# A planner's books for VectorE and GpSimd: one port booked for both, and GpSimd's measured durations

## The chip, the core and the metric

The kernel runs on one core of a Trainium2 chip. The metric is the device time of one execution in microseconds (us); the profile adds the span, which is the time from the first to the last instruction of the program. The engines are TensorE (PE in the profile, PEld for its weight loads), VectorE (DVE), ScalarE (ACT), GpSimd (POOL) and SyncE (SP), whose queue issues most DMAs.

## What is computed

The reference is a dynamic convolution followed by a mixture of experts with one expert for each token. There are 8 sequences of 3584 tokens with 192 values each, which makes 28,672 tokens. Cut to what matters:

```python
w = softmax(weight_gen)                         # [B, S, 8 heads, 7 taps]
out[b,s,h,:] = sum_k w[b,s,h,k] * x_pad[b, s+k, h,:]   # causal, 24 values per head
x = out.reshape(28672, 192)
e = argmax(x @ w_gate)                          # one of 8 experts
gate = softmax(x @ w_gate)[e]
eom = sigmoid(x @ w_output_gate)
out[token] = gate * eom[e] * (relu(x[token] @ w1[e]) @ w2[e])   # 192 -> 1024 -> 192
```

## The kernel before

**The work.** The convolution and the routing are done in 32 units of 896 tokens (128 partitions with 7 tokens each), here called units 0 to 31. For each unit the kernel normalizes the 7 tap weights, forms 7 products of shifted tokens and weights ("taps", 128x1344 elements each), adds them up, splits the sum into a high and a low float16 part in a buffer `rt`, computes the logits of both gates on TensorE, ranks the tokens by expert, and scatters the rows to the DRAM table `srtd`, which is sorted by expert. The scatter is seven GpSimd indirect DMAs for a unit ("sends", `srtd<-rt,posi`).

The experts run on "tiles" of 512, 384, 256 or 128 sorted rows, 81 in all. For a tile SyncE loads the row data (`meta` and the transposed `xT`) and the expert's weights (`wa`, 1024 KB, and `wb`, 768.5 KB, whatever the size of the tile). TensorE runs the first product into PSUM in 2, 4 or 8 pieces. Of each piece ScalarE makes `hh` (relu, float16) and VectorE makes `hl`, the rest that `hh` lost ("evacuation"). TensorE then runs the second product, ScalarE scales it to `ys`, and GpSimd writes the rows to their tokens with an indirect DMA (`out_dram<-ys,meta`).

**Who does the taps.** For units 0 to 6 GpSimd makes four taps (`gap`) and VectorE three (`vap`), and TensorE adds them in PSUM. From unit 7 on GpSimd makes five, VectorE makes two whose weights lie in PSUM, and VectorE adds all seven in PSUM. In the first part VectorE also splits the eight experts' weights into halves (`wpa`, `wpb`), which go back to DRAM as `wd` before any tile can load them.

**What sets the order.** Nothing of the order is written by hand. Each strand of the work is a Python generator ("chain"). `Order.step` picks the chain that can go on earliest by the planner's own books, and of equals the one with the lower rank: evacuations first, then outputs, placing, rounds, the units, and the expert products last. Each engine is wrapped by a `Paced` object, which keeps a booked time `t` for it and adds an estimated duration to it for every recorded instruction (`vector_cost`, `gpsimd_cost` and so on). So the estimates set in which order each engine gets its instructions, and SyncE its DMAs. On the chip each engine then executes that fixed list in order and waits where data are missing. The estimate has no other effect: the number of taps, tiles and evacuations is the same whatever it says.

After unit 31 the tiles that are left are put in an order that spreads the sizes (`mixed`). At that point a further pool of buffers for weights is opened, and the last table asks for eight writes of padding rows to `srtd` by SyncE (`srtd<-pad`). Two of VectorE's small instructions in each unit read two operands in SBUF: `ps<-base,done` and `ps<-zt`.

Of the kernel before, what the change touches and what calls it, by code (L numbers as in the profile page):

```python
# [14 lines left out]
ALU = mybir.AluOpType  # L15
# [52 lines left out]
class Chain:  # L68


    def __init__(self, gen, rank, t, engine):
        self.gen, self.rank, self.t, self.engine, self.gate = gen, rank, t, engine, None
        self.slack = EAGER[1] if len(rank) > 1 and rank[0] in EAGER[2] and rank[1] < EAGER[0] else SLACK


class Order:


    def __init__(self):
        self.now, self.chains = 0.0, []  # L80
        self.cur = Chain(None, (), 0.0, None)

    def add(self, gen, rank, engine, t=None):
# [23 lines left out]
class Queue:  # L107
# [12 lines left out]
    def __getattr__(self, name):  # L120
        f = getattr(self.engine, name)

        def call(*args, **kwargs):
            c, own, issue = self.order.cur, self.cost(name, args, kwargs), self.issue(name, args, kwargs)
            r = f(*args, **kwargs)  # L125
            if self.host is not None:
                self.issued = max(self.host.t, c.t)
                self.host.t = self.issued + issue
            self.issued = max(self.issued, self.order.now) + issue
            if own is not None:  # L130
                self.moved = max(self.moved, self.issued + 0.65) + own
                c.t = max(c.t, self.moved + 1.0)
            return r

        return call


class Paced:


    def __init__(self, order, engine, cost, before=0.0, after=None, lead=0.0, follows=True):
        self.order, self.engine, self.cost, self.t = order, engine, cost, 0.0
        self.before, self.after = before, LAT if after is None else after
        self.lead, self.follows = lead, follows

    def __getattr__(self, name):
        f = getattr(self.engine, name)

        def call(*args, **kwargs):
            c, own = self.order.cur, self.cost(name, args, kwargs)  # L150
            r = f(*args, **kwargs)  # L151
            if own is not None:
                self.t = max(self.t, (c.t if self.follows else self.order.now) + self.before) + own
                c.t = max(c.t, self.t + self.after)
            return r

        return call


def largest(args, kwargs):  # L160

    best = 1
    for o in (*args, *kwargs.values()):
        n = 1
        for v in getattr(o, "shape", ())[1:]:
            n *= v
        best = max(best, n)
    return best
# [10 lines left out]

def gpsimd_cost(name, args, kwargs):  # L180
    if name == "indirect_dma_start":
        return 1.04
    if name == "memset":
        return 1.0
    return 0.06 + largest(args, kwargs) * (0.0022 if kwargs.get("op") == ALU.add else 0.00174)


def tensor_cost(name, args, kwargs):
# [22 lines left out]
def kernel(ctx: ExitStack, tc: tile.TileContext, x, wg, wgate, wogate, w1, w2, cst, out):  # L211
    nc = tc.nc
    od = Order()
    V = Paced(od, nc.vector, vector_cost)
    S = Paced(od, nc.scalar, scalar_cost, after=LAT_S)
    G = Paced(od, nc.gpsimd, gpsimd_cost)
    T_ = Paced(od, nc.tensor, tensor_cost, after=0.0)
    SP = Queue(od, nc.sync, sync_cost, sync_issue, LEAD)
    TQ = SP if TURN_SP else Queue(od, nc.scalar, sync_cost, sync_issue, LEAD, S)
# [64 lines left out]
    def has(u, *what):  # L284
        return lambda: all(k in U[u] for k in what)
# [73 lines left out]
    def scattered(ins):  # L359

        tc.declare_no_dep(ins.ins, group="srt", reason="rows of its own")
        tc.add_to_no_dep_group("srt", ins.ins)
        state["writers"].append(ins.ins.name)
# [11 lines left out]
    def scales(ssq, sc, inv, name, free=None):  # L375

        n = ssq.shape[1]
        ex = sp.tile([P, n], I32, tag=f"ex{n}", name=f"ex_{name}")
        V.tensor_scalar(ex, ssq.bitcast(I32), 1, MASK, op0=ALU.arith_shift_right, op1=ALU.bitwise_and)
        if free is not None:  # L380
            free.append(od.cur.t)
        yield V
        V.tensor_scalar(sc.bitcast(I32), ex, -1.0, float(197 << 23), op0=ALU.mult, op1=ALU.add)
        V.tensor_scalar(inv.bitcast(I32), ex, float(57 << 23), None, op0=ALU.add)

# [3 lines left out]
    def gate_steps():  # L389
# [12 lines left out]
        T_.matmul(pg[:, 0:1], lhsT=ones32, rhs=gss, start=True, stop=True)  # L402
        yield V
        sg = cp.tile([P, 1], F32, name="sg")
# [6 lines left out]
        S.activation(gm[:, :, 0:16], g2, AF.Copy, scale=sg)  # L411
        yield V
        V.scalar_tensor_tensor(out=gm[:, :, 16:32], in0=g2, scalar=sg, in1=gm[:, :, 0:16], op0=ALU.mult, op1=ALU.subtract)
# [387 lines left out]
    def place_steps(u):  # L801
# [29 lines left out]
        d["placed"] = True  # L831
        yield G, has(u, "weighed")
        od.cur.t = max(od.cur.t, d["weighed_t"])
        for j in range(JS):
            yield G
            scattered(G.indirect_dma_start(
                out=srtd[:, :], out_offset=bass.IndirectOffsetOnAxis(ap=posi[:, j : j + 1], axis=0),
# [98 lines left out]
    def tile_load(t, T, ti, i, writers, ka, kb):  # L936
# [36 lines left out]
    def gemm2_group(d, g, at):  # L973
# [6 lines left out]
        for f in range(8):  # L980
# [215 lines left out]
```

## Time and profile before

| what | value |
|---|---|
| median of 3 runs | 1299.13 us |
| the three runs | 1295.3, 1299.13, 1304.6 us |
| the profiled execution's own time | 1304.16 us |
| its span | 1302.4 us |
| granted TensorE clock, mean | 0.968 |

The profiled execution is thus 5.0 us (0.4%) above the median of the runs. The profile's page gives busy times of each engine, a row of 40 slices of the span for each, the costliest groups of instructions, and the chain of work that ended last. Almost all instructions have line 151 of the kernel, which is the wrapper that records them; groups are told apart by the names of what they write and read. The instructions of units can be placed in time by VectorE's scan `p<-segs,ps`, of which there is one in each unit, just before the ranking. It is used below as a mark: "the scan of unit 7", "the scan of unit 31".

### The profile page before, as it was taken

The numbers are of one execution on the slowest core, as the hardware profiler recorded it, in microseconds if no ns is written. First come the engines' busy times: TensorE is split into PE (matmuls) and PEld (weight loads), VectorE is DVE, ScalarE is ACT, GpSimd is POOL, SyncE is SP. The second block draws the span as 40 slices with busy tenths as digits, with TensorE's granted clock in tenths as the row PEclk, the third lists the DMA queues.
The fourth block names the chain that finished last, engine by engine and source line by source line (L and its number), as shares of the span: only waits on it lengthen the run. The fifth ranks groups of instructions, "written<-read, shape, count | busy, mean of one in ns | idle before, by whom it ended". The sixth has DMA issues, their size and how long they took to land.

```text
span 1302.4 us, 28065 instructions
## 1 busy us (share of the span) xinstructions
PE 1147.5 (88%) x9958; PEld 834.1 (64%) x9958; DVE 1021.3 (78%) x2103; ACT 601.8 (46%) x1305; POOL 895.0 (69%) x776
## 2 busy tenths in 40 slices
PE   5886947898697988999997999989899999979998
PEld 2443426676464766676665766666566779878998
DVE  8898866999999999999999999999998633323332
ACT  3674642454353544554454554445454443434443
POOL 7689666667878887888898878998878534322222
PEclk9999878999898999999998999999999999999999
DMA  7777579889777977978797897768867899999994
GB/s 237 228 242 225 175 239 246 226 227 249 201 215 214 241 203 202 272 213 216 205 258 163 262 249 236 202 203 237 211 165 201 220 295 305 320 283 327 308 341 137
DMA packets 293853, 306.18 MB, mean 235 GB/s; under 512 B 232278, under 2 KB 253639, under 8 KB 283344
## 3 DMA queue, kind: packets, MB, share of 16 engines
q1 hardware_dynamic: 271728, 259.78, 70.7%
q0 software_dynamic: 21840, 44.30, 10.6%
q8 instruction: 78, 1.28, 0.4%
q14 instruction: 63, 0.52, 0.1%
q10 hardware_dynamic: 144, 0.31, 0.1%
HBM read 196.42 MB, written 62.01 MB: 198 GB/s over the span
## 4 chain that ended last, share of the span: by engine, by line
PE 38%; DVE 27%; POOL 10%; issue 10%; DMA 9%; ACT 3%; SPq 2%; POOLq 0%; DVEq 0%; ACTq 0%
PE ps L151 38%; DVE ps L151 13%; POOL gap L151 6%; DVE hl L151 4%; POOL srtd L151 3%; SPq L125 2%; DMA w<-in_wg_dram 2%; DVE vap L151 2%; DVE rt L151 2%; DMA wa<-wd 2%; POOL out_dram L151 2%; DMA srtd<-rt,posi 1%; ACT rt L151 1%; DVE w L151 1%; DVE vt L151 1%
## 5 line engine op out<-in xcount | busy, mean ns | idle before, releaser
L151 PE MATMUL ps<-xT,wa 128*128 128x512 f16 (+3 forms) x3240 | 561.1, 324 | 67.0 <-DVE hl L151 30.7
L151 PE MATMUL ps<-wb,hh 128*128 128x192 f16 x3696 | 479.6, 247 | 17.3 <-ACT ys L151 10.5
L151 DVE SCALAR_TENSOR_TENSOR hl<-ps,hh 128x512 f16<-128x512 f32 (+1 forms) x476 | 310.9, 666 | 191.4 <-ACT hh L151 188.3
L151 PE MATMUL ps<-wb,hl 128*128 128x192 f16 x1848 | 456.4, 247 | 0.0
L151 PEld LDWEIGHTS <-wa 128*128 128x128 f16 x3240 | 279.7, 99 | 259.3 <-issue 51.2
L151 POOL TENSOR_TENSOR gap<-x,w 128x960 f32<-128x960 f32 (+5 forms) x268 | 372.4, 1414 | 36.0 <-DVE w L151 13.3
L151 ACT ACTIVATE hh<-ps 128x512 f16<-128x512 f32 (+1 forms) x476 | 274.9, 583 | 229.3 <-PE ps L151 228.5
L151 PEld LDWEIGHTS <-hh 128*128 128x128 f16 x3696 | 337.7, 98 | 65.8 <-issue 25.1
L151 POOL DMA_INDIRECT out_dram<-ys,meta x216 | 214.3, 992 | 235.2 <-ACT ys L151 161.9
L151 POOL DMA_INDIRECT srtd<-rt,posi x224 | 230.0, 1027 | 90.7 <-issue 57.9
L151 ACT ACTIVATE ys<-ps,sc 128x192 f32<-128x192 f32 x231 | 97.1, 421 | 236.1 <-PE ps L151 153.5
L151 DVE TENSOR_TENSOR ps<-ps,gap 128x1344 f32<-128x1344 f32 x125 | 194.1, 1553 | 7.3 <-POOL gap L151 6.4
L151 PEld LDWEIGHTS <-hl 128*128 128x128 f16 x1848 | 181.7, 98 | 0.2
L151 POOL TENSOR_TENSOR gap<-halo,w 128x1152 f32<-128x1152 f32 (+4 forms) x38 | 62.4, 1642 | 18.9 <-issue 13.1
L151 PE MATMUL ps<-gap,cf 128*128 128x512 f32 x168 | 71.9, 566 | 2.7 <-POOL gap L151 2.7
L151 PE MATMUL ps<-vap,cf 128*128 128x512 f32 (+1 forms) x126 | 57.0, 596 | 13.1 <-DVE vap L151 13.1
L151 DVE SCALAR_TENSOR_TENSOR rt<-ps,sx,rt 128x448 f16<-128x448 f32 x64 | 57.6, 907 | 8.4 <-ACT rt L151 4.9
L151 PE MATMUL ps<-gm,gt 128*128 128x32 f16 x672 | 28.1, 177 | 41.0 <-ACT ys L151 12.3
L151 PEld LDWEIGHTS <-gt 128*128 128x128 f16 x672 | 25.2, 96 | 50.9 <-issue 35.7
L151 ACT ACTIVATE rt<-ps 128x1344 bf16<-128x1344 f32 x32 | 41.3, 1291 | 25.4 <-DVE ps L151 20.7
L151 PEld LDWEIGHTS ps<-gap,cf 128*128 128x128 f32 x168 | 31.3, 196 | 32.6 <-issue 26.8
L151 PEld LDWEIGHTS ps<-vap,cf 128*128 128x128 f32 x126 | 24.8, 208 | 36.8 <-issue 23.1
(115 smaller groups left out, 868.7 us busy)
## 6 DMA issues: line engine op xcount, KB each, us to landing
wa<-wd SPq DMA_DIRECT2D x81, 1024.0 KB
wb<-wd SPq DMA_DIRECT2D x81, 768.5 KB
x<-in_x_dram SPq DMA_DIRECT2D x32, 672.0 KB
w<-in_wg_dram SPq DMA_DIRECT2D x32, 196.0 KB
wd<-wpb SPq DMA_DIRECT2D x8, 768.5 KB
st<-in_w_dram SPq DMA_DIRECT2D x8, 768.0 KB
st<-in_w_dram SPq DMA_DIRECT2D x8, 512.0 KB
wd<-wpa SPq DMA_DIRECT2D x8, 512.0 KB
```

The lines of the kernel that those rows point to most:

```text
L125: r = f(*args, **kwargs)
L151: r = f(*args, **kwargs)
```

## The change

The books get one more entry, `port`: the time until which the two engines' common access to SBUF is taken. Every GpSimd instruction takes it. A VectorE instruction takes it if at least two of its tensor operands are not in PSUM. Such an instruction is booked to start no earlier than `port`, and `port` is then set to its end. GpSimd's durations are also booked longer: an indirect DMA at 1.2 us where it was 1.04 us, and a tap's product at 0.14 us and 0.00177 us for an element where it was 0.06 us and 0.00174 us. The program has the same instructions as before; only their order in the queues differs.

```diff
     def __init__(self):
-        self.now, self.chains = 0.0, []
+        self.now, self.chains, self.port = 0.0, [], 0.0
...
             if own is not None:
-                self.t = max(self.t, (c.t if self.follows else self.order.now) + self.before) + own
+                held = self.holds is not None and self.holds(kwargs)
+                self.t = max(self.t, (c.t if self.follows else self.order.now) + self.before, self.order.port if held else 0.0) + own
+                if held:
+                    self.order.port = self.t
                 c.t = max(c.t, self.t + self.after)
...
+def two_in_sbuf(kwargs):
+    return sum(k in kwargs and kwargs[k].space != bass.MemoryType.PSUM for k in ("in0", "in1", "data0", "data1")) > 1
...
 def gpsimd_cost(name, args, kwargs):
     if name == "indirect_dma_start":
-        return 1.04
+        return 1.2
...
-    return 0.06 + largest(args, kwargs) * (0.0022 if kwargs.get("op") == ALU.add else 0.00174)
+    return 0.14 + largest(args, kwargs) * (0.0022 if kwargs.get("op") == ALU.add else 0.00177)
...
-    V = Paced(od, nc.vector, vector_cost)
+    V = Paced(od, nc.vector, vector_cost, holds=two_in_sbuf)
...
-    G = Paced(od, nc.gpsimd, gpsimd_cost)
+    G = Paced(od, nc.gpsimd, gpsimd_cost, holds=lambda kwargs: True)
```

Three places show how the order moves.

The first is GpSimd's queue where the taps of unit 7 begin (`gap7_0`; `posi4` and `posi5` are the positions of units 4 and 5, so these rows are sends). Before:

```order
L151 TENSOR_TENSOR gap6_3_1363<-x6_825,w6_821 128x768
L151 DMA srtd_81<-rt_0_102,posi3_1237 230528x194 x2
L151 DMA srtd_81<-rt_1_104,posi4_1472 230528x194 x7
L151 DMA srtd_81<-rt_2_106,posi5_1659 230528x194
L151 TENSOR_TENSOR gap7_0_1725<-x6_825,w7_964 128x1152
L151 TENSOR_TENSOR gap7_0_1725<-x7_973,w7_964 128x192
```

With the change, the same place:

```order
L151 TENSOR_TENSOR gap6_3_1539<-x6_840,w6_835 128x768
L151 DMA srtd_81<-rt_1_104,posi4_1405 230528x194
L151 TENSOR_TENSOR gap7_0_1571<-x6_840,w7_1105 128x1152
L151 TENSOR_TENSOR gap7_0_1571<-x7_1107,w7_1105 128x192
L151 DMA srtd_81<-rt_1_104,posi4_1405 230528x194
L151 TENSOR_TENSOR gap7_1_1621<-x6_840,w7_1105 128x960
```

The taps of unit 7 now stand before and between the sends of unit 4 and not behind all of them and one of unit 5.

The second place is TensorE's queue at the ranking of unit 31, the last unit (`p3_31` is its scan's result; `hl44_7` is the last evacuated piece of tile 44, `xT45` the rows of tile 45). Before:

```order
L151 LDWEIGHTS hl44_7_14413
L151 MATMUL ps_85<-wb44_13952,hl44_7_14413 128x192
L151 LDWEIGHTS upper_97
L151 MATMUL ps_85<-p3_31_14659,upper_97 128x8
L151 LDWEIGHTS ones16_100
L151 MATMUL ps_85<-p3_31_14659,ones16_100 128x8
L151 LDWEIGHTS wa45_14199
L151 MATMUL ps_85<-xT45_14197,wa45_14199 128x512
```

With the change:

```order
L151 LDWEIGHTS hl45_7_14625
L151 MATMUL ps_85<-wb45_14241,hl45_7_14625 128x192
L151 LDWEIGHTS upper_97
L151 MATMUL ps_85<-p3_31_14872,upper_97 128x8
L151 LDWEIGHTS ones16_100
L151 MATMUL ps_85<-p3_31_14872,ones16_100 128x8
L151 LDWEIGHTS wa46_14345
L151 MATMUL ps_85<-xT46_14343,wa46_14345 128x512
```

Exactly one more tile of 512 rows stands ahead of the last unit's ranking, and one fewer behind it.

The third place is SyncE's queue in the tail, at the loads of tile 56 (`ti30`, `ti31` are tables of units 30 and 31). Before:

```order
L125 TENSOR_LOAD ti30_0_14290
L125 ISA x3
L125 DMA meta56_16053<-srtd_81 128x4x2
L125 ISA
L125 DMA_TRANSPOSE xT56_16055<-srtd_81 128x3x512
L125 ISA
L125 DMA wa56_16057<-wd_82 128x2048
L125 ISA
L125 DMA wb56_16059<-wd_82 128x1537
```

With the change:

```order
L125 TENSOR_LOAD ti31_1_15120
L125 ISA x3
L125 DMA meta56_16231<-srtd_81 128x2x2
L125 ISA
L125 DMA_TRANSPOSE xT56_16233<-srtd_81 128x3x256
L125 ISA
L125 DMA wa56_16235<-wd_82 128x2048
L125 ISA
L125 DMA wb56_16237<-wd_82 128x1537
```

Tile 56 has 256 rows now and not 512. By the same listing the sizes from the first small tile to the second 512 behind the padding writes were 128, 256, 128, 128, 128, 256, 128, **512**, 128, 128, 256, 128, the eight padding writes, 128, 128, **512** (tiles 49 to 63). They are now 128, 256, 128, 128, 128, 256, 128, 128, 128, 256, 128, the padding writes, 128, 128, **512** (tiles 51 to 64): two tiles of 512 more were taken before the mixed part, and thirteen small tiles stand in a row. Behind that, one run of sixteen small tiles stands where there were two of eight with a 512 between them.

More of the change, by code (lines that the diff above doesn't have):

```diff
@@ L138, with __init__ @@
 class Paced:
-    def __init__(self, order, engine, cost, before=0.0, after=None, lead=0.0, follows=True):
+    def __init__(self, order, engine, cost, before=0.0, after=None, lead=0.0, follows=True, holds=None):
         self.order, self.engine, self.cost, self.t = order, engine, cost, 0.0
         self.before, self.after = before, LAT if after is None else after
-        self.lead, self.follows = lead, follows
+        self.lead, self.follows, self.holds = lead, follows, holds
     def __getattr__(self, name):
```

## The prediction

> **What bounds the kernel now.** I read the page first: span, busy times, slices.
>
> ```profile
> span 1302.4 us, 28065 instructions
> PE 1147.5 (88%) x9958; PEld 834.1 (64%) x9958; DVE 1021.3 (78%) x2103; ACT 601.8 (46%) x1305; POOL 895.0 (69%) x776
> PE   5886947898697988999997999989899999979998
> DVE  8898866999999999999999999999998633323332
> POOL 7689666667878887888898878998878534322222
> DMA  7777579889777977978797897768867899999994
> ```
>
> The profiled execution took 1304.16 us, 1.8 us more than its span and 5.0 us more than the median of 1299.13 us. All sums below are differences, and I put them on the median at the end. The slices show two regimes. VectorE stands at nine tenths for most of the first 31 slices and at two or three afterwards; TensorE is nine throughout the last eight, where DMA is nine as well. To find the border I took VectorE's scans of units 7 and 31 from the timeline, and then the busy times by stretch.
>
> ```profile
> 273.18 0.27 DVE L151 TENSOR_TENSOR_SCAN p<-segs,ps 128x56 f16<-128x56 f16 x1
> 1024.37 0.26 DVE L151 TENSOR_TENSOR_SCAN p<-segs,ps 128x56 f16<-128x56 f16 x1
> ...
> core 0: us, PE busy (x) PEld busy (x) DVE busy (x) ACT busy (x) POOL busy (x), PEclk, DMA share, GB/s
> 0.00:273.20 273.20, 204.13 (x1140) 123.83 (x1141) 224.27 (x436) 135.38 (x258) 187.07 (x143) 0.91 0.76 229
> 273.20:1024.40 751.20, 677.27 (x5832) 479.07 (x5831) 702.11 (x1481) 358.79 (x820) 621.82 (x546) 0.98 0.81 218
> 1024.40:1302.40 278.00, 266.12 (x2991) 231.24 (x2988) 94.91 (x189) 107.66 (x229) 86.06 (x88) 0.99 0.90 288
> ```
>
> In the opening (273 us) no engine is full: VectorE 224 us, GpSimd 187 us. In the middle (751 us) VectorE is busy 702 us or 93%, TensorE 90%, GpSimd 83% without the gaps between its DMAs. In the tail (278 us) TensorE is busy 266 us and DMA has a share of 0.90. What ends the waits in the middle is read from the chain of work within it.
>
> ```profile
> by line: PE ps L151 28.7%; DVE ps L151 21.4%; issue 9.7%; DVE hl L151 7.5%; POOL gap L151 6.5%; POOL srtd L151 3.0%; POOL out_dram L151 2.9%; DVE rt L151 2.8%; DMA w<-in_wg_dram 2.3%; SPq L125 1.5%; DVE vt L151 1.4%; DMA x<-in_x_dram 1.2%;
> ```
>
> The rows that begin with DVE make 33%, TensorE 29%, GpSimd's three 12%. So nothing rules the middle alone: work added to an engine there costs roughly its share of the chain.
>
> **Opening, to the scan of unit 7.** The change moves work here without adding any. Counted in TensorE's order, 215 first-product and 240 second-product matmuls of tiles stand ahead of the ranking of unit 7, where there were 235 and 288; VectorE evacuates 28 pieces (12,288 columns), not 33 (14,208). The price of a piece is in the groups, with GpSimd's two kinds of work:
>
> ```profile
> L151 DVE SCALAR_TENSOR_TENSOR hl<-ps,hh 128x512 f16<-128x512 f32 x420 | 281.5, 682 | 190.1 <-ACT hh L151 187.1 <-issue 2.4
> L151 POOL TENSOR_TENSOR gap<-x,w 128x960 f32<-128x960 f32 (+5 forms) x268 | 372.4, 1414 | 36.0 <-DVE w L151 13.3 <-issue 11.4 <-PE ps L151 8.6
> L151 POOL DMA_INDIRECT out_dram<-ys,meta x216 | 214.3, 992 | 235.2 <-ACT ys L151 161.9 <-issue 20.2 <-ACT hh L151 9.5
> ```
>
> 1,920 columns fewer are 3.75 pieces at 682 ns, or -2.6 us; I take that, since VectorE is the busiest here. In GpSimd's queue two taps of unit 7 now stand ahead of the last send of unit 4. A tap is two instructions of 1,414 ns, so a send can come up to 5.7 us later, and with it the tiles that wait for its rows. That is the upper end. The lower end is what the two engines lose to each other here:
>
> ```profile
> L151 DVE SCALAR_TENSOR_TENSOR wpa<-st,wsc,wpa 128x1024 f16<-128x1024 f32 x8 | 24.9, 3118 | 1.0 <-ACT wpa L151 0.7 <-DMA st<-in_w_dram 0.3
> L151 DVE SCALAR_TENSOR_TENSOR wpb<-st,wsc,wpb 128x1536 f16<-128x1536 f32 x8 | 20.4, 2555 | 1.1 <-ACT wpb L151 1.1
> L151 DVE TENSOR_TENSOR vap<-x,w 128x1344 f32<-128x1344 f32 x7 | 14.0, 1996 | 0.0
> ...
> 120.65 9.07 DVE L151 SCALAR_TENSOR_TENSOR wpa<-st,wsc,wpa 128x1024 f16<-128x1024 f32 x1 [0.18 <-ACT wpa L151]
> 120.61 8.03 POOL L151 TENSOR_TENSOR gap<-x,w 128x1152 f32<-128x1152 f32 x6
> 174.56 1.81 DVE L151 SCALAR_TENSOR_TENSOR wpb<-st,wsc,wpb 128x1536 f16<-128x1536 f32 x1
> ```
>
> A `wpb` that met nobody took 1.81 us, the mean is 2.56 us: 8 times 0.75 is 6.0 us. A `wpa` by the same rate would take 1.21 us against 3.12 us: 15.3 us. `vap` at 1344 elements by that rate 1.58 us against 2.00 us: 2.9 us. Together 24.2 us are lost, so the opening's ends are -27 and +6 us, and the value -2.6 us, because the order still lets taps follow taps in GpSimd's queue.
>
> **Middle, unit 7 to unit 31.** Here the order does add work: one tile of 512 rows more stands ahead of unit 31, and the opening gave some up. From the same counts TensorE gets 55,808 columns more and VectorE 6,016 (11.75 pieces), and GpSimd 7 writes of rows (152 against 145 between the last sends of units 8 and 31). The speed of TensorE on tiles of 512 alone is seen early in the tail, beside later rows that are used below:
>
> ```profile
> 1050.00:1070.00 20.00, 20.00 (x164) 14.09 (x163) 6.43 (x10) 8.10 (x16) 5.71 (x6) 1.00 1.06 340
> 1150.00:1170.00 20.00, 13.81 (x202) 13.13 (x200) 4.35 (x7) 5.82 (x13) 3.91 (x4) 1.00 0.99 290
> 1190.00:1210.00 20.00, 20.00 (x276) 19.67 (x275) 6.92 (x10) 8.09 (x17) 4.55 (x5) 1.00 0.92 297
> 1270.00:1290.00 20.00, 20.00 (x262) 19.55 (x259) 6.92 (x10) 8.47 (x20) 4.00 (x5) 1.00 0.62 212
> ```
>
> 164 matmuls in 20.00 us, 136 in a tile: 16.6 us for the 38,912 columns of a tile of 512, so 8.3 us for one of 256 and 4.15 us for one of 128 rows. The middle's additions are 23.8 us of TensorE, 8.0 us of VectorE, 7 times 992 ns or 6.9 us of GpSimd. If only VectorE counted, the cost would be 8.0 us, if TensorE did, 23.8 us. By the chain's shares it is 0.29 x 23.8 + 0.33 x 8.0 + 0.12 x 6.9 = 10.4 us, and I take that.
>
> The two small VectorE instructions that wait for GpSimd in each unit stay where their unit is. They are why the books were changed, so I looked at what they meet:
>
> ```profile
> L151 DVE TENSOR_TENSOR ps<-base,done 1x8 f32<-1x8 f32 x31 | 32.4, 1045 | 0.9
> ...
> 336.49 5.24 DVE L151 TENSOR_TENSOR ps<-base,done 1x8 f32<-1x8 f32 x1
> 336.34 5.36 POOL L151 TENSOR_TENSOR gap<-x,w 128x960 f32<-128x960 f32 x4
> ...
> 379.24 0.17 DVE L151 TENSOR_TENSOR ps<-base,done 1x8 f32<-1x8 f32 x1
> 378.74 1.01 POOL L151 DMA_INDIRECT out_dram<-ys,meta  x1 [0.17 <-issue]
> ```
>
> One waited through four products of GpSimd in a row; the other ran in 0.17 us beside a DMA of GpSimd. So the books are wrong twice, too short against taps and too long against sends. Nothing in them moves these instructions away from taps, because `port` is not part of what `step` compares: 0 us for them. [...]
>
> **Tail, after the scan of unit 31.** One tile of 512 fewer is -16.6 us if TensorE stays fed. What feeds it:
>
> ```profile
> wa<-wd SPq DMA_DIRECT2D x81, 1024.0 KB
> wb<-wd SPq DMA_DIRECT2D x81, 768.5 KB
> srtd<-pad SPq DMA_DIRECT2D x9, 97.0 KB
> ...
> 1133.56 0.41 SPq L125 DMA_DIRECT2D wa<-wd  x1
> 1135.31 10.34 SPq L125 DMA_DIRECT2D srtd<-pad  x8
> 1149.04 0.35 SPq L125 DMA_DIRECT2D meta<-srtd  x1
> ...
> 1155.67 6.42 DMA wa<-wd
> 1165.21 5.24 DMA wa<-wd
> ```
>
> Each tile loads 1,792.5 KB of weights; 128 rows add 97 KB in and 98 KB out (128 x 192 values of 4 bytes). That is 1,988 KB for a tile of 128 and 2,183 KB for one of 256. At the 340 GB/s of the row from 1050 us, where DMA is full, these are 5.85 and 6.42 us, against 4.15 and 8.3 us of TensorE. So small tiles run the store of loaded tiles down, and a 512 fills it. The store is three tiles behind the one in work (four `xT` buffers): 12.45 us, less 5.2 to 6.4 us for a load to land, is 6.6 us. Before, four small tiles stand between the 512 and the padding writes; DMA needs 24.0 us for them, TensorE 20.75 us, and TensorE then waits behind the writes (6.42 and 5.24 us). With the change eleven small tiles (eight of 128, three of 256) stand ahead of the writes: 66.0 against 58.1 us. The deficit is 7.9 us and not 3.2 us, so 4.7 us more are waited. Of the later run of sixteen (twelve and four) DMA needs 95.9 us, TensorE 83.0 us; less the store, 6.3 us are waited. The two runs of eight that stood there have a deficit of 6.4 us each, just inside the store, and in the rows from 1190 and 1270 us, which lie in them, TensorE is never idle. The tail is -16.6 + 4.7 + 6.3 = -5.6 us. Its ends are -16.6 us, if DMA keeps up, and the second rival's.
>
> **Sum.** -2.6 + 10.4 - 5.6 = +2.2 us: 1306.4 us on the profiled execution's own time, 1301.3 us on the median, +0.2%.
>
> **Rivals.** *The opening gets shorter.* If the new order keeps the two-operand instructions and the taps apart, the 24.2 us go as well: 1301.3 - 24.2 = 1277 us. It decides, at under 1286.1 us, from 15.2 of the 24.2 on. For it speaks that no engine is full in the opening, so that its time goes to waits; against it the waits over several taps, and that `step` does not look at `port`.
>
> *The tail starves (slower).* At the 290 GB/s of the row from 1150 us, a tile of 128 takes 6.86 us and one of 256 takes 7.53 us. The eleven then need 77.5 us, 19.4 over; the four of before are 7.4 over; the sixteen need 112.4 us, 29.4 over, less the store 22.8. That is 12.0 + 22.8 = 34.8 us in place of 11.0: 1301.3 + 23.8 = 1325 us. It decides, at over 1312.1 us, from 10.8 us more than in the sum. For it speaks that DMA is full in the tail; against it that at 290 GB/s the two runs of eight would have waited 8 us each before, which they did not.
>
> *TensorE sets the middle.* Then the middle costs 23.8 us and not 10.4 us: 1314.7 us. For it speaks that TensorE is busy 90% there and gets most of the addition; against it that VectorE is busier.
>
> *The books change nothing that counts.* The middle hides its additions in its waits, and the tail loses what it gains: 1299 us.
>
> **How the numbers follow.** A measurement of this kernel can tell about 1% from no change. The sum and the last rival together get 0.50, the first rival 0.22, the second 0.14 and the third 0.14. The sum's own range, with each term between its nearer bounds (opening -2.6 to +5.7, middle 8.0 to 15.0, tail -10.0 to -2.0), is 1295 to 1318 us. The range over the cases is 1278 to 1324 us. Faster by over 1% gets 0.22, within 1% 0.50, slower by over 1% 0.28.
>
> **What would show it.** The opening: the scan of unit 7 near 270 us, and the mean of `wpa` at 1024 still near 3 us (the first rival: below 2 us, and the scan below 258 us). The middle: 762 us between the scans (third rival: 775 us). The tail: 272 us after the scan of unit 31, with TensorE's waits for `wa` grown from 11.7 us to about 23 us, behind the padding writes and in the last run (second rival: 46 us). I would be wrong about the middle if the distance of the scans shrank although a tile was added, since then the order's waits and not its work set it.

## The result, and the profile after

The changed kernel takes 1332.07 us in the median of 4 runs (1329.67 to 1338.26), the kernel before beside it 1298.93 us (4 runs). The ratio is 1.0258, 95% interval 1.0205 to 1.0312: slower, and outside the predicted range of 1278 to 1324 us. The profiled execution took 1329.88 us. Its page begins so:

```profile
span 1328.1 us, 28053 instructions
PE 1154.5 (87%) x9958; PEld 838.9 (63%) x9958; DVE 1014.3 (76%) x2103; ACT 604.5 (46%) x1305; POOL 898.0 (68%) x776
PE   6877586998897999887989787999998999978998
DVE  7997779899997999898999789799998553322331
POOL 6867678837887878877878868788888444411222
```

The busy times are those of before within 1%: most of the time went into waits. The three stretches show where. First the two scans that mark them, then the busy times in the same columns as before:

```profile
267.36 0.26 DVE L151 TENSOR_TENSOR_SCAN p<-segs,ps 128x56 f16<-128x56 f16 x1
1055.58 0.26 DVE L151 TENSOR_TENSOR_SCAN p<-segs,ps 128x56 f16<-128x56 f16 x1
```

```profile
0.00:267.40 267.40, 197.18 (x1060) 116.23 (x1061) 221.46 (x427) 131.75 (x249) 198.93 (x150) 0.90 0.74 225
267.40:1055.60 788.20, 705.98 (x6049) 501.13 (x6047) 703.76 (x1499) 371.68 (x841) 616.91 (x542) 0.97 0.79 214
1055.60:1328.10 272.50, 251.34 (x2855) 221.52 (x2852) 89.08 (x181) 101.06 (x216) 82.16 (x84) 0.98 0.89 283
```

The opening is 5.8 us shorter (267.4 against 273.2) and the tail 5.5 us shorter (272.5 against 278.0). The middle is 37.0 us longer: 788.2 against 751.2. Cut once more at the scans of units 15 and 23, the middle is, before:

```profile
273.20:522.60 249.40, 214.89 (x1844) 152.83 (x1843) 237.15 (x489) 114.73 (x272) 201.85 (x177) 0.96 0.82 218
522.60:775.00 252.40, 232.61 (x2014) 164.39 (x2013) 237.17 (x510) 124.73 (x280) 216.27 (x189) 0.99 0.84 226
775.00:1024.40 249.40, 229.78 (x1979) 161.85 (x1977) 227.79 (x485) 119.33 (x270) 203.70 (x181) 0.99 0.78 209
```

and after:

```profile
267.40:522.00 254.60, 226.43 (x1975) 162.99 (x1973) 233.75 (x506) 122.54 (x285) 191.37 (x169) 0.98 0.82 223
522.00:808.90 286.90, 250.29 (x2098) 175.88 (x2097) 253.46 (x517) 130.11 (x291) 227.54 (x199) 0.96 0.75 206
808.90:1055.60 246.70, 229.26 (x1982) 162.27 (x1980) 216.56 (x476) 119.03 (x267) 197.99 (x176) 0.97 0.81 215
```

The first third takes 131 matmuls more in 5.2 us more. The second takes 84 more, half a tile and a little, and is 34.5 us longer; the third gives 2.7 us back. So the loss does not lie where most of the added work lies. TensorE's idle time in the second third went from 19.8 to 36.6 us, its clock from 0.99 to 0.96. What TensorE waited for over the whole middle (us in total, times, longest), before and then after:

```profile
PE ps L151 <- DVE hl L151: 26.2, 20, 4.8
PE ps L151 <- ACT ys L151: 23.0, 30, 2.3
PE ps L151 <- DMA wa<-wd: 11.3, 2, 6.5
```

```profile
PE ps L151 <- DMA wa<-wd: 30.5, 7, 8.4
PE ps L151 <- DVE hl L151: 23.2, 19, 3.2
PE ps L151 <- ACT ys L151: 21.2, 30, 3.7
```

The waits for a tile's weights grew by 19.2 us; the others shrank by 10.9 us in sum. So TensorE's idle time in the middle grew by 8.3 us only (73.9 to 82.2 us), and its busy time by 28.7 us, of which the added work is 23.8 us by the prediction's rate. In the chain of waits within the middle, by line, TensorE's share was 28.7% and that of SyncE's queue 1.5%; now it reads

```profile
by line: PE ps L151 44.3%; DVE ps L151 15.3%; issue 6.7%; DVE hl L151 6.0%; DMA wa<-wd 3.9%; SPq L125 3.3%; POOL gap L151 3.0%; DMA w<-in_wg_dram 1.8%; POOL srtd L151 1.8%; DVE rt L151 1.6%; DMA out_dram<-ys,meta 1.4%; POOL out_dram L151 1.
```

The three long waits of the second third are alike: ahead of each SyncE had waited for `rt`, 15.5, 18.7 and 17.0 us. This is the first, ahead of tile 24, in SyncE's queue:

```profile
601.60 6.36 SPq L125 DMA_TRANSPOSE gt<-rt  x4
609.85 0.41 SPq L125 DMA_DIRECT2D meta<-srtd  x1
612.10 0.40 SPq L125 DMA_DIRECT2D wa<-wd  x1
```

with the wait of SyncE that ends there:

```profile
SPq L125 <- DVE rt L151: 15.5, 1, 15.5
```

and in TensorE's:

```profile
618.68 1.89 PE L151 MATMUL ps<-xT,wa 128*128 128x512 f16 x4 [5.54 <-DMA wa<-wd]
```

These are the busy times of four stretches of 3.5 us, behind waits of 5.07, 5.54, 8.41 and 7.31 us for `wa` (the granted clock is the number behind POOL's):

```profile
402.60:406.10 3.50, 3.50 (x9) 1.29 (x10) 3.42 (x5) 0.60 (x1) 3.30 (x4) 0.50 1.19 206
618.70:622.20 3.50, 3.50 (x9) 1.29 (x10) 3.30 (x7) 0.60 (x1) 3.16 (x3) 0.50 1.28 219
760.20:763.70 3.50, 3.50 (x30) 1.61 (x29) 0.65 (x2) 1.13 (x3) 3.31 (x3) 0.59 1.18 208
828.10:831.60 3.50, 3.47 (x29) 1.69 (x30) 1.86 (x2) 1.09 (x3) 3.33 (x3) 0.54 1.16 299
```

A unit's four transposes stand in SyncE's queue until VectorE has written `rt`, here until 601.6 us; the loads of tile 24 stand behind them, and TensorE, which has one tile loaded ahead (tile 23, in work from 593.4 us), runs dry at 613.1 us. After such a wait it works 3.5 us at about half speed: the clock is 0.50 to 0.59. In the 9.80 us behind the second of the four stretches it was 0.95.

### The profile page after: what moved, and what is told of

Read it like the earlier page. It is cut to its first block, busy times and chain, and to the rows that moved or that the text cites. A ratio compares the mean times of both kernels' runs of the same rounds, so it can differ in the third digit from the quotient of the medians.

```text
span 1328.1 us, 28053 instructions
## 1 busy us (share of the span) xinstructions
PE 1154.5 (87%) x9958; PEld 838.9 (63%) x9958; DVE 1014.3 (76%) x2103; ACT 604.5 (46%) x1305; POOL 898.0 (68%) x776
## 3 DMA queue, kind: packets, MB, share of 16 engines
q8 instruction: 78, 1.28, 0.4%
## 4 chain that ended last, share of the span: by engine, by line
PE 49%; DVE 24%; DMA 9%; issue 5%; POOL 5%; ACT 4%; SPq 3%; POOLq 0%; DVEq 0%; ACTq 0%
PE ps L151 49%; DVE ps L151 11%; DMA wa<-wd 5%; DVE hl L151 4%; POOL gap L151 3%; SPq L125 3%; DVE vap L151 2%; DVE rt L151 1%; DMA w<-in_wg_dram 1%; POOL srtd L151 1%; ACT rt L151 1%; DVE vt L151 1%; DMA out_dram<-ys,meta 1%; POOL out_dram L151 1%; DVE w L151 1%
## 5 line engine op out<-in xcount | busy, mean ns | idle before, releaser
L151 POOL TENSOR_TENSOR gap<-x,w 128x960 f32<-128x960 f32 (+5 forms) x268 | 372.4, 1415 | 40.4 <-DVE w L151 20.7
L151 PEld LDWEIGHTS <-hh 128*128 128x128 f16 x3696 | 338.4, 99 | 59.2 <-issue 19.8
L151 POOL DMA_INDIRECT srtd<-rt,posi x224 | 233.2, 1041 | 102.9 <-issue 54.1
L151 PE MATMUL ps<-vap,cf 128*128 128x512 f32 (+1 forms) x126 | 64.4, 656 | 26.5 <-DVE vap L151 26.5
L151 POOL TENSOR_TENSOR gap<-halo,w 128x1152 f32<-128x1152 f32 (+4 forms) x38 | 62.2, 1636 | 6.7 <-DVE w L151 5.3
L151 DVE TENSOR_TENSOR vap<-x,w 128x960 f32<-128x960 f32 (+4 forms) x31 | 62.2, 2031 | 0.0
```

## Experiments

Two theories stood at the start. The first: the change put transposes that wait for a late `rt` ahead of tile loads in SyncE's queue. The second, the prediction's third rival: TensorE sets the middle, and the added 55,808 columns cost their full 23.8 us. A third was formed after the first runs: the tiles are asked for too close behind the sends of their rows.

The runs fell into five jobs on several chips. The kernel before took 1304.6 and 1303.9 us in two jobs (the parts; TensorE's work, second pair), and 1361.7, 1360.7 and 1367.4 us in the three others. Most of that difference lies in the middle: the program of after_less_pe, which ran in both kinds, took 807.2 and 787.7 us there. So only ratios within a job are compared. The changed kernel itself ran beside the others only in the two jobs of the first kind. Twice it was the control:

> The changed kernel once more, as the control for the runs beside it. Both theories: 1.02 to 1.03 of the kernel before.

> The changed kernel as the control beside the three others: 1.02 to 1.03.

It measured 1.0261 (1.0202 to 1.0319) and 1.0242 (1.0204 to 1.0281).

### The price of TensorE's work alone

No queue changes its order here. Work is added to the kernel before:

```diff
             T_.matmul(py, lhsT=hh, rhs=w2l, start=False, stop=False)
-            T_.matmul(py, lhsT=hl, rhs=w2h, start=False, stop=(f == 7))
+            more = 22 <= t < 31
+            T_.matmul(py, lhsT=hl, rhs=w2h, start=False, stop=(f == 7 and not more))
+            if more:
+                nc.tensor.matmul(py, lhsT=hl, rhs=w2h, start=False, stop=(f == 7))
```

or taken from the changed one, where the books still count it:

```diff
-            T_.matmul(py, lhsT=hl, rhs=w2h, start=False, stop=(f == 7))
+            if less:
+                T_.t += 192 / 2400.0 + 6 / 2400.0
+            else:
+                T_.matmul(py, lhsT=hl, rhs=w2h, start=False, stop=(f == 7))
```

> The kernel before, with the same product of tiles 22 to 30 done twice: 55,296 columns more for TensorE in the middle and no queue in another order. The output holds that part twice. This is the price of the added work by itself. Second theory (TensorE's pace, and the prediction's third rival): 23.7 us longer, near 1323 us. First theory (and the prediction's weighting): 0.29 of it, 7 us, so 1303 to 1309 us.

> The changed kernel, without the third of the three second products (hl with the upper half of w2) of tiles 22 to 30: 55,296 columns fewer for TensorE, about what the change put more before unit 31, while every queue keeps its order and VectorE still evacuates hl. The output lacks that part of the second product. Second theory (TensorE's pace): 23.7 us shorter, near 1308 us, and 764 us between the scans of unit 7 and unit 31. First theory (the queue): the long waits end when the late transposes end, whatever TensorE does before, so what is saved there turns into longer waits; by the chain's share of 0.29 it is 7 us, at most 12, so 1320 to 1327 us.

They measured 1.0032 (0.9991 to 1.0074) and 0.9998 (0.9960 to 1.0036). The first speaks against the second theory; the second says nothing without the changed kernel beside it, so both were run again in a job with that control:

> The kernel before with 55,296 columns of TensorE more in the middle (the hl product of tiles 22 to 30 twice; the output holds it twice), no queue in another order. If TensorE's work sets the middle: 1.018. If its price is the chain's share: 1.005. The earlier run gave 1.003 [0.999, 1.007].

> The changed kernel without 55,296 columns (the hl product of tiles 22 to 30 is left out of the output), no queue in another order. If TensorE's work sets the middle: 0.018 below the control, 1.008. If its price is the chain's share: 0.005 below the control, 1.021.

Adding the work costs a factor of 1.0083 (1.0042 to 1.0123), that is 10.8 us (5.5 to 16) for 23.7 us of TensorE. Taking it away gives 1.0223 (1.0181 to 1.0264), 0.0019 below its control and within its interval; 0.018 was the second theory's number. The middles of the control (after_control_2) and of the kernel with less work (after_less_pe_2), each with TensorE's waits, show where the saving went. The control:

```profile
266.70:1057.70 791.00, 703.56 (x6049) 500.06 (x6048) 704.00 (x1499) 371.84 (x841) 616.76 (x542) 0.97 0.79 213
```

and its waits:

```profile
PE ps L151 <- DMA wa<-wd: 34.6, 7, 9.9
PE ps L151 <- DVE hl L151: 22.2, 18, 3.5
```

With less work:

```profile
266.60:1054.30 787.70, 685.57 (x5761) 477.68 (x5759) 701.34 (x1499) 370.29 (x841) 616.76 (x542) 0.96 0.79 214
```

and its waits:

```profile
PE ps L151 <- DMA wa<-wd: 41.0, 8, 11.0
PE ps L151 <- DVE hl L151: 28.3, 23, 4.8
```

TensorE is busy 18.0 us less, and waits 6.4 us longer for weights and 6.1 us longer for `hl`. The second theory falls: the middle of the changed kernel does not go at TensorE's pace.

### The parts of the change

port_alone has the old durations, durations_alone the new ones without the port, port_taps takes GpSimd's DMAs out of the port, and nudge_dma changes one estimate of the kernel before by 10 ns:

```diff
-        return 1.2
+        return 1.04
...
-    return 0.14 + largest(args, kwargs) * (0.0022 if kwargs.get("op") == ALU.add else 0.00177)
+    return 0.06 + largest(args, kwargs) * (0.0022 if kwargs.get("op") == ALU.add else 0.00174)
```

```diff
-        return 1.04
+        return 1.2
...
-    return 0.06 + largest(args, kwargs) * (0.0022 if kwargs.get("op") == ALU.add else 0.00174)
+    return 0.14 + largest(args, kwargs) * (0.0022 if kwargs.get("op") == ALU.add else 0.00177)
```

```diff
-    G = Paced(od, nc.gpsimd, gpsimd_cost, holds=lambda kwargs: True)
+    G = Paced(od, nc.gpsimd, gpsimd_cost, holds=lambda kwargs: "out_offset" not in kwargs)
```

```diff
-        return 1.04
+        return 1.05
```

> Only the port is booked; GpSimd's durations are the old ones. If the port is what costs (it books VectorE's two-operand instructions behind sends, beside which they ran in 0.17 us), this is slower by 2 to 3% and the durations alone are within 1%. If the fault is only in which of many orders came out, this is slower by 1 to 3% as well, and so is each of the other two.

> Only GpSimd's longer durations; no port. If the port is what costs, within 1% of before. If the durations are, slower by 2 to 3%. If only the order that came out counts, slower by 1 to 3%.

> The change, but GpSimd's DMAs do not take the port, as the rows of 0.17 us beside them say. If the false holding behind sends is what costs, within 1% of before. If only the order that came out counts, slower by 1 to 3%.

> The kernel before, with one estimate changed that means nothing: a DMA of GpSimd at 1.05 us instead of 1.04 us. The opening's order stays; from there on it differs, and VectorE has 349 pieces ahead of unit 31's scan, four fewer than before. If what the books say is what counts, within 0.5% of before. If the order before is one of few good ones and any other costs its waits, slower by 1 to 3%.

The table holds the ratios and, from the profiled execution of each, the three stretches (opening, middle, tail, us), VectorE's pieces in the middle, and TensorE's waits for `wa` there. In the last column are those of tiles 10 to 44 whose `meta` load was issued less than 3 us after the end of the last send of the unit in whose table the tile stands, that is at once when its rows had landed.

| kernel | ratio (95%) | stretches | pieces | wa waits | loads at once |
|---|---|---|---|---|---|
| before | 1 | 273.2, 751.2, 278.0 | 320 | 11.3 | 3 of 35 |
| nudge_dma | 1.0045 (1.0015 to 1.0074) | 273.7, 749.1, 288.1 | 316 | 26.9 | 2 |
| port_taps | 1.0160 (1.0096 to 1.0224) | 255.9, 792.1, 271.4 | 339 | 20.8 | 6 |
| after | 1.0258 (1.0205 to 1.0312) | 267.4, 788.2, 272.5 | 333 | 30.5 | 8 |
| durations_alone | 1.0287 (1.0225 to 1.0350) | 258.6, 802.7, 271.4 | 333 | 40.5 | 6 |
| port_alone | 1.0358 (1.0289 to 1.0428) | 284.3, 785.0, 276.1 | 319 | 43.3 | 9 |

port_alone, durations_alone and port_taps ran beside after_control (1.0261), nudge_dma beside after_control_2 (1.0242). Neither the port nor the durations are to blame by themselves: each alone costs about as much as both together, or more. That sends take the port too may cost up to 1% (1.0160 against 1.0261), but without it the change is still slower. A nudge that means nothing costs 0.45%. That is within the 0.5% expected if it is what the books say that counts, and below the 1 to 3% expected if any other order costs its waits; so one other order, at least, is nearly as good as the one before. All four larger changes lengthen the middle by 34 to 52 us. The clearest row is port_alone: its middle has one piece fewer than the kernel before, and still is 33.8 us longer.

```profile
284.30:1069.30 785.00, 689.38 (x5852) 485.32 (x5851) 700.92 (x1486) 363.50 (x822) 614.46 (x541) 0.96 0.79 211
```

TensorE's waits there:

```profile
PE ps L151 <- DMA wa<-wd: 43.3, 6, 12.3
```

Its matmuls are about as many as before (5,852 to 5,832), TensorE waits 32.0 us more for weights, and its clock fell from 0.98 to 0.96. So the middle can grow by this much with no added work at all.

SyncE's queue shows what changed. In the middle it waited 126.4 us for sends before and 138.8 us with the change, and 156.8 and 162.4 us for `rt`, at the longest 18.7 us in both; so neither sum changed much. But a load in this kernel waits for every send that is recorded ahead of it, and not only for those of its own rows. Sorted by the unit of the send that ended the wait, those for the unit of the tile's own table were 40.1 us before and 35.6 us in nudge_dma, but 93.9 us with the change, 74.9 us in port_taps, 67.6 us in durations_alone and 118.6 us in port_alone. The rest, 86.3 us before and 45.0 us with the change, were for sends of later units, which hold none of the tile's rows. Such waits of SyncE need not reach TensorE, which has a tile loaded ahead: before, SyncE waited 283.2 us for sends and `rt` in the middle, and TensorE 11.3 us for `wa`.

### Transposes behind the loads

In SyncE's queue alone, the transposes of a unit are issued behind the next tile's loads; the books are unchanged.

```diff
-            for n in range(0, 4 * JS, 7):
-                TQ.dma_start_transpose(out=turned[:, n : n + 7, :], in_=flat[:, n * P : (n + 7) * P])
+            turn = lambda q: [q.dma_start_transpose(out=turned[:, n : n + 7, :], in_=flat[:, n * P : (n + 7) * P]) for n in range(0, 4 * JS, 7)]
+            if u in (18, 22, 24):
+                TQ.booking = True
+                turn(TQ)
+                TQ.booking = False
+                held.append(lambda: turn(nc.sync))
+            else:
+                turn(TQ)
...
+            while held:
+                held.pop(0)()
```

With `booking` set the queue only books. What is held is issued behind the next tile's loads, or at the unit's logits if those come first. swap_all has `u >= PE_U` (7) in place of the three units.

> The changed kernel, with the four transposes of units 18, 22 and 24 in SyncE's queue moved behind the loads of tiles 24, 31 and 34, which stood right behind them; the books and every other queue are as with the change. First theory (the queue): the loads waited there behind transposes that waited 15.5 to 18.7 us for VectorE's rt, so TensorE's three waits of 5.5, 8.4 and 7.3 us go, and the run is 15 to 21 us shorter than with the change, near 1311 to 1317 us. Second theory (TensorE's pace): the middle is as long as TensorE's work there, which is the same, so the next wait takes the place of each and the run stays within 8 us of 1332 us.

> As swap_three, for every unit from 7 on: its four transposes are issued behind the next tile's loads if such loads come before the unit's logits in the program. Where rt was in time, the transposes now come later by the loads' issue, 2 to 3 us. First theory: at least the gain of swap_three, 1305 to 1317 us. Second theory: 1324 us or more.

swap_three measured 1.0103 (1.0029 to 1.0178) and swap_all 1.1079 (1.0996 to 1.1162), both in a job without the changed kernel. What SyncE waited for between 600 and 640 us in swap_three, and then the issue of tile 24's loads and of the transposes that now follow:

```profile
SPq L127 <- DMA srtd<-rt,posi: 17.6, 1, 17.6
```

```profile
618.08 0.34 SPq L127 DMA_DIRECT2D meta<-srtd  x1
620.65 0.38 SPq L127 DMA_DIRECT2D wa<-wd  x1
621.76 9.88 SPq L684 DMA_TRANSPOSE gt<-rt  x4
```

With the transposes out of the way, SyncE's queue waited about as long (17.6 us, where it had waited 15.5 us for `rt`), and the transposes then took 9.88 us of issue. The wait was not for the tile's own rows: tile 24 stands in the table of unit 16, whose last send had ended at 608.7 us, and the wait ended behind a send of unit 17 that began at 615.38 us. At the loads of tiles 31 and 34 the queue waited for sends, too, 20.7 us and twice, 14.4 and 7.3 us. So the transposes hid a second wait at all three places. TensorE nevertheless waited less for these tiles' `wa` (0, 3.5 and 6.1 us in place of 5.5, 8.4 and 7.3 us), but it now waited for `gt`, for which the waits view of the changed kernel's middle has no row:

```profile
PE ps L153 <- DMA gt<-rt: 13.3, 10, 6.5
PE ps L153 <- DMA wa<-wd: 12.9, 3, 6.1
```

Whether the run is 15 to 21 us shorter than the changed kernel, as the first theory expected, cannot be told without that kernel in the job. In swap_all `gt` is TensorE's largest wait in the middle:

```profile
PE ps L153 <- DMA gt<-rt: 128.2, 61, 10.2
```

In these two runs, what was put second in this queue is what TensorE waited for next. The first theory is half right: the transposes hold the loads back, but so do the sends behind them.

### Sends and writes in GpSimd's queue

Here a unit's seven sends are issued in one row, at the place of the first:

```diff
         for j in range(JS):
             yield G
-            scattered(G.indirect_dma_start(
...
+            for i in range(JS) if u >= PE_U and j == 0 else (j,):
...
+                if i > j:
+                    sent.append(nc.gpsimd.indirect_dma_start(**kw))
```

> The changed kernel, with the seven sends of every unit from 7 on in one row in GpSimd's queue, at the place of the first; taps and writes of results that stood between them come behind. The books and all other queues are as with the change. Third theory (late rows: TensorE waits for a tile whose rows GpSimd has not yet sent, since its sends stand between taps and writes, 25.5 us from the first to the end of the last): rows are there some 15 us sooner, the waits for wa go, and the ratio to the kernel before falls from 1.026 to 1.000 to 1.012. First theory (late transposes in SyncE's queue): VectorE's rt comes no sooner, the ratio stays at 1.02 to 1.03. Second theory (TensorE's pace): 1.02 to 1.03.

> The same row of seven sends in the kernel before, where the first to the end of the last took 22.6 us and TensorE waited 11.3 us for wa in the middle. Third theory: a small gain, 0.985 to 1.000, since few waits are there to be saved, less what the taps lose by coming up to 7 us later. First and second theory: 0.995 to 1.01.

and here the writes of results before the end of unit 31 take a tile that was filled at the start:

```diff
-            send(d["meta"][:, g, 1:2], d["ys"][:, g, :])
+            send(d["meta"][:, g, 1:2], d["ys"][:, g, :] if "all" in state else still)
```

> The changed kernel, but until the last unit is through GpSimd's writes of results take their rows from a tile that was filled at the start and not from ys, so that no write waits for ScalarE and no ys waits for a write; all queues keep their order. The output lacks the results of those tiles. With the change GpSimd waited for ys 33 times and 43.3 us before those writes in the middle (before: 10 times, 14.9 us), and the sends stand behind them. Third theory, in its form as a ring (late TensorE, late ys, late write, late sends, late rows, late TensorE): most of the loss comes round this way, and the ratio falls to 0.985 to 1.008. First and second theory: not below 1.015.

> The same in the kernel before, as the control. If the writes' waits are what sets the two kernels apart, this gains at most 10 us (0.99 to 1.00) and comes out within 1% of the changed kernel with the same edit. If not, the two stay 2% or more apart.

The results are 1.0610 (1.0560 to 1.0661) and 1.0530 (1.0485 to 1.0574) with the sends first, 1.0192 (1.0145 to 1.0238) and 1.0280 (1.0238 to 1.0323) with free writes. All four miss what the third theory expected of them. The first two miss the other expectations, too; after_free_writes is where the other two theories had it (not below 1.015). From the first send of a unit to the end of the last it took 8.7 us (22.6 and 25.5 us without the edit), and the waits for `wa` in the middle of the kernel before nearly vanished (0.2 us), but others came in their place. TensorE's waits in the middle of after_sends_first:

```profile
PE ps L151 <- ACT ys L151: 60.3, 43, 5.1
PE ps L151 <- issue: 38.9, 32, 4.9
PE ps L151 <- DMA wa<-wd: 18.0, 5, 8.5
```

Seven sends in a row stand ahead of the writes that free `ys`, and the waits for `ys` are 60.3 us; that the one makes the other was not tested. The 38.9 us under "issue" have no releaser in the records and stay unexplained. Free writes settle nothing about the ring through late writes. The two kernels came out within 1% of each other, the changed one 0.9% ahead, which is what was expected if the ring sets them apart; but neither gained by the edit, and how far apart the unedited kernels are in this job was not measured. Why an edit that only takes waits away makes the kernel before 2.8% slower is open.

### Rows that are always there

```diff
         rows = srtd[bass.ds(row, T), :]
+        if t >= 8 and "all" not in state:
+            rows, writers = own[0:T, :], []
...
+            for j in range(4):
+                nc.gpsimd.dma_start(out=own[j * P : (j + 1) * P, :], in_=d["ri"][:, j, 0:W])
```

> The changed kernel, but the tiles from 8 on that are loaded before the last unit is through read the 512 rows of unit 0, which are kept in a table of their own, and so wait for no later send; results go to consecutive rows. The output is thus not that of the true rows. Engines' orders stay, but for four small DMAs on GpSimd in the opening. Third theory (late rows): TensorE's waits for wa in the middle fall from 30.5 us to under 12 us, and the ratio to the kernel before from 1.025 to 1.000 to 1.010. First theory (late transposes ahead of the loads in SyncE's queue): they stand there still, 1.018 to 1.028. If the order as such costs in many small waits: 1.015 to 1.025.

> The same edit in the kernel before, as the control. Third theory: 0.990 to 1.000, since its rows are mostly there when they are asked for, and at most 1% from the changed kernel with the same edit. The other two: the two stay 1.5% or more apart.

The changed kernel measured 0.9889 (0.9848 to 0.9931), the kernel before 0.9981 (0.9955 to 1.0007). Their middles and TensorE's waits for weights, first of after_free_rows:

```profile
272.80:1077.70 804.90, 707.90 (x6048) 502.83 (x6047) 703.37 (x1498) 367.80 (x841) 615.75 (x542) 0.97 0.80 210
```

and

```profile
PE ps L151 <- DMA wa<-wd: 21.3, 4, 7.9
```

then of before_free_rows:

```profile
273.10:1074.30 801.20, 689.31 (x5828) 487.99 (x5827) 695.05 (x1480) 354.80 (x819) 621.33 (x546) 0.96 0.77 206
```

and

```profile
PE ps L151 <- DMA wa<-wd: 5.8, 1, 5.8
```

With rows that need no waiting the two middles differ by 3.7 us and not by 37, and the changed kernel keeps the gains of its opening and tail. Taken alone this is what the third theory says, though 0.9889 is below all three ranges that were expected. Three things hold it back. The waits for `wa` fell to 21.3 us and not under 12 us as expected: the three long ones of the second third are still there (3.8, 7.9 and 7.7 us), behind the same transposes, so for these late rows are not needed. These waits still differ by 15.5 us between the two kernels, while the middles differ by 3.7 us. And in this kind of job the distance of the two unedited kernels was not measured. The same program with less TensorE work was 2.25% lower against the kernel before in such a job (0.9998 against 1.0223), so the changed kernel may lie near 1.00 there even without the edit. No run took away both the late transposes and the late rows.

## Why the prediction was wrong

**Opening: right.** Predicted -2.6 us, measured -5.8 us, inside its ends. The sign that I named for it was wrong, though: the mean of `wpa` at 1024 was to stay near 3 us. It fell to 1.92 us, below the 2 us that I had named for the first rival, and `vap` rose (`wpa` and `wpb` by shape, `vap` all shapes):

```profile
L151 DVE SCALAR_TENSOR_TENSOR wpa<-st,wsc,wpa 128x1024 f16<-128x1024 f32 x8 | 15.3, 1924 | 1.5 <-ACT wpa L151 1.5
L151 DVE SCALAR_TENSOR_TENSOR wpb<-st,wsc,wpb 128x1536 f16<-128x1536 f32 x8 | 14.8, 1847 | 0.6 <-ACT wpb L151 0.5
L151 DVE TENSOR_TENSOR vap<-x,w 128x960 f32<-128x960 f32 (+4 forms) x31 | 62.2, 2031 | 0.0
```

`wpa` at 1024 and `wpb` together lost 15.2 us (45.3 to 30.1 us). `vap` over all its shapes gained 14.6 us, from 47.6 us before to 62.2 us. The collisions with GpSimd did not go; they moved from the weights to the taps, so the first rival had no gain to show. The traces show it: `wpa` and `wpb` of all shapes ran 31.1 us beside products of GpSimd before and 16.7 us after, `vap` 31.5 us before and 43.7 us after. The `wpa` at 1024 that met a product took 3.38 us in the mean before (seven of eight) and 2.31 us after (five), the others 1.27 and 1.28 us.

**Small port instructions: wrong, and without effect.** I put 0 us for the two that wait in each unit. `ps<-base,done` fell from 32.4 to 25.3 us, `ps<-zt` from 24.5 to 23.3 us:

```profile
L151 DVE TENSOR_TENSOR ps<-base,done 1x8 f32<-1x8 f32 x31 | 25.3, 817 | 1.0
```

No run shows that the port did this: 14 of the 31 `ps<-base,done` met a product of GpSimd before, and 17 did after. Those took 2.12 us in the mean before and 1.35 us after, the others 0.16 and 0.17 us, also the six and eight of them that ran beside a DMA of GpSimd (0.16 and 0.17 us). These durations are what the traces show of the common access that the books call `port`; that it is one, and to SBUF, is the books' assumption and was not shown. The drop nearly pays for the 8.0 us of added pieces: VectorE was busy 703.8 us in the middle after 702.1 us. But VectorE's idle time there went from 49.1 to 84.4 us, so the saving went into waits.

**Middle: wrong.** Predicted +10.4 us, measured +37.0 us. The step that failed is "work added to an engine there costs roughly its share of the chain", taken as the whole price of the new order. As a price of work it held: 23.7 us of TensorE alone cost 10.8 us (5.5 to 16), where the share of 0.29 gives 6.9 us, and the third rival's 23.8 us is outside that interval. After the change the chain's share did not give the price: TensorE has 44.3% of it, 10.5 us for 23.7 us of work, and 2.5 us were saved (0.0019 of 1303.9 us; by the four runs of each, from 6.6 us saved to 1.6 us lost). What was left out is what the order does to waits. More tiles of the middle now stand close behind the sends of their rows (8 of 35 loads at once, not 3), and the three longest waits of TensorE stand behind transposes that waited for `rt`. I counted the columns that moved and not the distance from producer to consumer that they used up, though the loads' place behind transposes in SyncE's queue was to be read from the order. By TensorE's time the 37.0 us are 23.8 us of work, 4.9 us more of busy time, which goes with the lower clock (0.98 to 0.97), 19.2 us of added waits for `wa`, less 10.9 us of other waits that went. This sum is an account and no proof: it does not say what would be left without one of its terms. Shown by runs is that such work costs at most 16 us in the order before, and that an order with no added work (port_alone) loses 33.8 us in the middle.

**Tail: right, in part by luck.** Predicted -5.6 us, measured -5.5 us. The added waits for `wa` after the scan of unit 31 were to be 11.0 us; they are 9.3 us, at the places that I named: 6.4 us about the padding writes, for which I had 4.7 us, and 3.0 us in the last run, for which I had 6.3 us. TensorE's busy time fell by 14.8 us and not by 16.6 us, and the two misses cancel. The 11.7 us that I gave for before were two DMA rows of the chain and not waits of TensorE; the waits view counts 6.7 us. Before:

```profile
PE ps L151 <- DMA wa<-wd: 6.7, 3, 4.0
```

and after:

```profile
PE ps L151 <- DMA wa<-wd: 16.0, 7, 7.4
```

**Range.** Its upper end came from a starving tail. No case stood for a middle that waits, so the range ended 8 us short of the time.

**What stays open.** The waits are shown, and that neither the added work, nor the port, nor the durations by themselves are their cause. That late rows are what most of them come down to is supported by the column of loads at once (2 and 3 in the two fast orders, 6 to 9 in the four slow ones) and by SyncE's waits for a tile's own rows (36 to 40 us and 68 to 119 us), but not settled: the three longest waits stand behind transposes, and the free rows have no control. nudge_dma, with 26.9 us of waits for `wa` in a middle of 749.1 us, shows that these waits alone do not give the time: VectorE was busy 20 us less there. So the cause of the 37.0 us is narrowed down and not shown.

## What to carry to other kernels

A change to estimates that orders the queues is not priced by the work that it moves past a mark: for each consumer, count how far behind its producer it now stands in every queue, and price the waits where that margin is gone. Booked durations nearer to the measured ones need not give a better order (1.0287 here with them alone); change each part alone and nudge an estimate by nothing before blaming or praising a part. Run the unedited kernel beside its edits in every job, or the ratios cannot be read. In the changed kernel's middle a wait of TensorE of 5.07 to 8.41 us cost more than itself, since the clock was 0.50 to 0.59 in the 3.5 us behind it.

## What the hardware showed beside that

- Behind each of the changed kernel's four waits of 5.07 to 8.41 us in the middle, TensorE's granted clock was 0.50 to 0.59 over 3.5 us; 4 matmuls of 512 columns took 1.89 us there, and by the 16.6 us of a tile's 38,912 columns they would take 0.87 us.
- Four DMA transposes of a unit took SyncE's queue 9.00 to 10.31 us at the seven places in the changed kernel's middle where they were issued within 1.25 us behind a tile's `wb`, and 5.31 to 7.86 us at the other seventeen. In swap_three, right behind the loads of tile 24, they took 9.88 us.
- The ratio of two programs was not the same on two chips. The same program with less TensorE work was at 0.9998 of the kernel before in a job where that took 1361.7 us, and at 1.0223 where it took 1303.9 us. On the first chip, the slower one, TensorE waited 41.6 us for `ys` in the middle, on the other 19.6 us.
